# The last leftover sum of an attention and feed-forward kernel: its last step, its copy and its stores by halves of the columns

## The chip, the cores and the metric

The kernel runs on one core of a Trainium2 chip. The metric is the device time of one execution in microseconds (us); the text names the median of a few runs and, where the trace is read, the one execution that the profiler recorded. The engines are called as the profile calls them: PE (TensorE, the matrix products; PEld its weight loads), DVE (VectorE), ACT (ScalarE), POOL (GpSimd) and SP (SyncE). SP and ACT also issue transfers (DMAs), each on a hardware queue of its own: q1 is SP's, q10 is ACT's. The packets of both queues are carried by the core's 16 DMA engines. Below, an "engine" is a compute engine unless "DMA engine" is said.

## The reference

For each of 8 batches, attention over 32 memory slots makes a matrix x of 576 rows and 512 columns, and a two-layer feed-forward net follows on all 4608 rows:

```
x = attention(q, k, v, phi)          # 8 batches of 576 rows, 512 columns
h = x @ w_in                         # 2048 columns
g = 0.5 * h * (1 + erf(h / sqrt(2)))
out = g @ w_out                      # 4608 x 512, float32
```

## The kernel before

The second product, `g @ w_out`, sums over 2048 hidden columns in 16 steps f of 128 (`NF` = 16). Each step is three matmuls (`products`, L938), since g and w_out are each split in a high and a low part. The rows go in tiles of 128. From each half of a batch (288 rows), 256 rows go through `project_half`, and 32 rows are left over. The leftover rows of two batches, four blocks of 32, are gathered in the tile `tails` and make one tile of 128 rows: the leftover sum `tacc`, one bank of PSUM with 512 columns. It is made by `tail_split` (DVE splits `tails` in a high and a low part, four steps f at a time), `tail_project` (PE, 16 steps of three matmuls) and `tail_evict` (a copy of `tacc` from PSUM to the tile `to` in SBUF, and the stores of `to` to `out`). The last such sum, of batches 6 and 7 (b = B - 1 = 7), is the last work of the program: when its copy and its stores are done, the program ends.

In `out` the four blocks of 32 rows lie apart: block x starts at row (b - 1) * 576 + 288 x + 256, and a row is 2048 B. For b = 7 one 32-row store is issued for each block, in turn on ACT's and SP's queue (L1021). For b = 3 and b = 5 all four blocks go in one store (L1025), for b = 1 there are two stores of 64 rows (L1029). Another transfer that comes up below is the small load of `aT` (L473): it reads 64 rows as two blocks of columns, [2, 64, 128], from memory. The names `DMAHW0_49` and so on in the rows of the program's order are semaphores of transfers, `PE_49`, `DVE_49` and `Activation_49` those of the engines' work.

The order of the instructions on each engine is fixed by the program: a list written by hand, and then a plan.

Of the kernel before, what the change touches and what calls it, by code (L numbers as in the profile page):

```python
# [149 lines left out]
def slot_attention_gelu_ffn(  # L150
# [30 lines left out]
    nc = tc.nc  # L181
    P = 128
    B, G, _, S = phiT.shape
    M = 32
    D = P // 2
    NF, _, DM = w_in.shape
    DFF = NF * P
    HS = S // 2
# [41 lines left out]
    for x in PLACES.split():  # L230
        tag, size, n = x.replace("*", ":").split(":")
        sb.tile([P, int(size) // 4], F32, tag=tag, name=f"place_{tag}", bufs=int(n))

    def home(name):
        return {"tag": homes[name], "name": name, "bufs": 1}

    st = {"engine": None}

    def eng(usual):
        return {"d": nc.vector, "a": nc.scalar, "p": nc.gpsimd}[st["engine"] or usual]  # L240

    def copy(usual, dst, src):
        e = eng(usual)
        return e.copy(dst, src) if e is nc.scalar else e.tensor_copy(dst, src)  # L244
# [641 lines left out]
    def g_of(w, *k):  # L886

        dt, n = {"gf": (F32, 2), "gh": (F32R, 2), "gl": (F32R, 2)}[w]
        k = (w, *k)
        return tile_of(  # L890
            k, lambda: gs.tile([P, MAIN], dt, tag=w, name="_".join(map(str, k)), bufs=n)
        )
# [43 lines left out]
        nc.vector.tensor_copy(gh, x)  # L936
        nc.vector.tensor_tensor(gl, x, gh.bitcast(F32), op=ALU.subtract)

    def products(acc, f, gh, gl, first, last):
        for n, (x, w) in enumerate(((gh, wo_hi), (gh, wo_lo), (gl, wo_hi))):  # L940
            nc.tensor.matmul(  # L941
                acc, x, w[:, f, :], start=(first and n == 0), stop=(last and n == 2)
            )

    def project(b, f):
        _, _, first, last = steps[at_step[b, f]]
        if first:
            st["acc"] = [
                ps_acc.tile([P, DM], F32, tag=f"acc{j}", name=f"acc_{b}_{f}_{j}")
                for j in range(NT)  # L950
            ]
        acc = st["acc", b, f] = st["acc"]
        gh, gl = g_of("gh", b, f), g_of("gl", b, f)
        for j in range(NT):
            js = slice(j * P, (j + 1) * P)
            products(acc[j], f, gh[:, js], gl[:, js], first, last)

    def project_half(b, hf, i):
        if i == 0:
            st["acc", b, hf] = [  # L960
                ps_acc.tile([P, DM], F32, tag=f"acc{j}", name=f"acc_{b}_{hf}_{j}")
                for j in range(2)
            ]
        acc = st["acc", b, hf]
        gh, gl = g_of("gh", b, hf, i), g_of("gl", b, hf, i)
        for j in range(2):
            for x in range(2):
                js = slice((2 * x + j) * P, (2 * x + j + 1) * P)
                f = 2 * i + x
                products(acc[j], f, gh[:, js], gl[:, js], f == 0, f == NF - 1)  # L970
# [13 lines left out]
    def tail_project(b, k):  # L984
        if k == 0:
            st["tacc", b] = ps_acc.tile([P, DM], F32, tag="acc0", name=f"tacc_{b}")
        gh, gl = (g_of(w, "t", b, k) for w in ("gh", "gl"))
        for n in range(4):
            js = slice(n * P, n * P + P)
            f = 4 * k + n  # L990
            products(st["tacc", b], f, gh[:, js], gl[:, js], f == 0, f == NF - 1)

    def evict(b, j, f):

# [19 lines left out]

    def tail_evict(b):
        o = sb.tile([P, DM], F32, **home(f"to_{b}"))
        copy("a", o, st["tacc", b])
        if b == B - 1:
            for x in range(4):
                r = (b - 1) * S + x * HS + 2 * P  # L1020
                (nc.scalar, nc.sync)[x % 2].dma_start(out[r : r + M, :], o[M * x : M * x + M])  # L1021
            return
        if b > 1:
            rows = out[(b - 1) * S : (b + 1) * S].rearrange("(x s) n -> x s n", s=HS)
            nc.sync.dma_start(rows[:, 2 * P :], o)  # L1025
            return
        for x in range(2):
            r = (b - 1 + x) * S + MAIN
            nc.sync.dma_start(out[r : r + TL, :], o[TL * x : TL * x + TL])  # L1029
# [14 lines left out]
        "h": hidden, "gelu": gelu, "gh": gelu_hi, "gl": gelu_lo, "p": project, "o": evict, "os": store,  # L1044
        "P": project_half, "O": evict_half,
        "tg": tail_split, "tp": tail_project, "to": tail_evict,
    }
    st.update({("far", "pu", b, f): 1 for b in range(3, B) for f in (4, 12)})
# [27 lines left out]
    n = 2 * NF  # L1076
# [69 lines left out]
    for b, t in times.items():  # L1146
        x = 4 if b == 3 else b + 2
# [36 lines left out]
    first = {}  # L1184
# [46 lines left out]
    last = {}  # L1231
# [43 lines left out]
```

## Time and profile before

| | before |
|---|---|
| median of 3 runs | 699.79 us (699.37 to 701.95) |
| the profiled execution's own time | 700.24 us |
| its span, from the first instruction to the last | 698.5 us |
| PE busy | 684.2 us, 98% of the span |
| DVE, ACT, POOL busy | 54%, 43%, 6% |
| mean granted TensorE clock, share of full speed | 0.991 |
| bytes moved by DMA | 64.37 MB, mean 92 GB/s |

The profiled execution is 1.74 us longer than its span, and 0.45 us above the median. A change at the program's end moves the span's end by what it moves the last landing. Two measurements of this kernel can tell differences of about 0.5%, 3.5 us.

### The profile page before, as it was taken

To read this page: it belongs to the slowest core of one execution; us is meant where nothing else is said; L and a number is where in the kernel's file an instruction comes from. 1 tells how busy PE (TensorE), PEld (TensorE's weight loads), DVE (VectorE), ACT (ScalarE), POOL (GpSimd) and SP (SyncE) were. 2 spreads that over 40 slices of the span, in tenths; PEclk is the share of its full clock that TensorE was granted. 3 is DMA by queue.
4 is the path that set the end of the run, shared out by engine and by line. 5 is a ranking of instruction groups with operands and counts; after the bars stand their busy time and mean duration, and the time that the engine had idled before them with its cause. 6 is when DMAs were issued, how large, how long until landed. Compare 5 with 4: busy or idle time off the path is not lost.

```text
span 698.5 us, 12349 instructions
## 1 busy us (share of the span) xinstructions
PE 684.2 (98%) x4942; PEld 569.0 (81%) x4942; DVE 376.4 (54%) x695; ACT 301.3 (43%) x781; POOL 45.3 (6%) x38
## 2 busy tenths in 40 slices
PE   6799999999999999999999999999999999999997
PEld 5577887888768888888887888888878888888886
DVE  3999868854683555434844256334734246432222
ACT  5989658444652443615553234232531225332220
POOL 1333143300000000000000000000000000000000
PEclk9799999999999999999999999999999999999999
DMA  9973255322347260164501100030000200000001
GB/s 323 378 291 121 95 216 131 121 89 95 99 136 214 77 207 1 65 183 142 164 1 49 65 2 31 1 99 1 30 1 31 84 1 31 1 31 0 31 1 45
DMA packets 30717, 64.37 MB, mean 92 GB/s; under 512 B 3780, under 2 KB 8644, under 8 KB 30660
## 3 DMA queue, kind: packets, MB, share of 16 engines
q1 hardware_dynamic: 30564, 63.46, 27.3%
q8 instruction: 39, 0.64, 0.4%
q10 hardware_dynamic: 96, 0.13, 0.1%
q14 instruction: 18, 0.15, 0.1%
HBM read 54.13 MB, written 9.44 MB: 91 GB/s over the span
## 4 chain that ended last, share of the span: by engine, by line
PE 92%; DMA 4%; ACT 2%; SPq 1%; issue 0%; POOL 0%; ACTq 0%
PE acc L941 50%; PE h L901 28%; PE tacc L941 6%; PE pu L619 4%; DMA raw<-w_out 2%; DMA kv<-kv 1%; DMA raw<-w_in 1%; PE psc L619 1%; PE psc L536 1%; PE x L536 1%; ACT phi L432 0%; PE pt L457 0%; PE pk L536 0%; SPq L288 0%; ACT aT L244 0%
## 5 line engine op out<-in xcount | busy, mean ns | idle before, releaser
L901 PE MATMUL h<-p_hi,U 128*128 128x288 f32 x1024 | 202.1, 297 | 0.2 <-ACT tails L922 0.2
L941 PE MATMUL acc<-wo_hi,gh 128*128 128x512 f32 x512 | 201.0, 393 | 0.0
L941 PE MATMUL acc<-wo_lo,gh 128*128 128x512 f32 x512 | 199.6, 390 | 0.0
L941 PE MATMUL acc<-wo_hi,gl 128*128 128x512 f32 x512 | 199.5, 390 | 0.0
L913 ACT ACTIVATE gf<-h 128x256 f32<-128x256 f32 x192 | 74.0, 387 | 262.8 <-issue 182.2
L901 PEld LDWEIGHTS h<-p_hi,U 128*128 128x128 f32 x1024 | 163.3, 188 | 19.7 <-issue 7.3
L244 DVE CAST gh<-gf 128x512 fp32r<-128x512 f32 x106 | 45.0, 424 | 183.1 <-ACT gf L913 168.7
L941 PEld LDWEIGHTS acc<-wo_hi,gh 128*128 128x128 f32 x512 | 96.4, 188 | 23.9 <-issue 4.3
L941 PEld LDWEIGHTS acc<-wo_hi,gl 128*128 128x128 f32 x512 | 96.1, 188 | 20.9 <-DVE gl L928 0.5
L941 PEld LDWEIGHTS acc<-wo_lo,gh 128*128 128x128 f32 x512 | 96.1, 188 | 15.9
L901 PE MATMUL h<-p_lo,U 128*128 128x288 f32 x512 | 108.6, 294 | 0.0
L928 DVE TENSOR_TENSOR gl<-gf,gh 128x512 fp32r<-128x512 f32 x128 | 90.5, 708 | 24.1 <-ACT gh L244 14.8
L901 PEld LDWEIGHTS h<-p_lo,U 128*128 128x128 f32 x512 | 81.2, 188 | 0.2 <-DVE p_lo L739 0.2
L860 DVE TENSOR_TENSOR U<-pu,U 128x512 fp32r<-128x512 f32 (+2 forms) x50 | 40.8, 835 | 34.9 <-ACT U L244 34.7
L915 ACT ACTIVATE tails<-h 128x32 f32<-128x32 f32 x192 | 37.3, 194 | 0.0
L619 PE MATMUL pu<-w_in_sb,kT 64*32 64x512 f32 (+2 forms) x624 | 34.4, 528 | 1.0 <-ACT kT L244 0.6
L244 ACT CAST U<-pu 128x512 fp32r<-128x512 f32 (+2 forms) x43 | 28.9, 707 | 8.6 <-PE pu L619 7.4
L941 PE MATMUL tacc<-wo_hi,gh_t 128*128 128x512 f32 x64 | 25.3, 395 | 0.0
L941 PE MATMUL tacc<-wo_hi,gl_t 128*128 128x512 f32 x64 | 24.9, 390 | 0.0
L941 PE MATMUL tacc<-wo_lo,gh_t 128*128 128x512 f32 x64 | 24.9, 389 | 0.0
L342 POOL TENSOR_TENSOR y<-y,raw 128x512 int32<-128x512 int32 x14 | 18.8, 1346 | 58.4 <-DVE raw L318 25.3
L342 POOL TENSOR_TENSOR w_in_sb<-y,raw 128x512 int32<-128x512 int32 x14 | 20.4, 1465 | 29.3 <-DVE raw L318 8.0
(126 smaller groups left out, 571.5 us busy)
## 6 DMA issues: line engine op xcount, KB each, us to landing
kv<-kv SPq DMA_DIRECT2D x48, 256.0 KB, 5.7
out<-o SPq DMA_DIRECT2D x16, 512.0 KB, 4.4
raw<-w_out SPq DMA_DIRECT2D x14, 512.0 KB, 7.1
raw<-w_in SPq DMA_DIRECT2D x14, 512.0 KB, 9.7
q<-qT SPq DMA_DIRECT2D x9, 576.0 KB, 5.4
phi<-phiT SPq DMA_DIRECT2D x16, 288.0 KB, 3.5
aT<-phiN SPq DMA_DIRECT2D x6, 512.0 KB, 3.5
q<-qT SPq DMA_DIRECT2D x10, 288.0 KB, 8.6
```

The costliest lines, as they stand in the source:

```text
L244: return e.copy(dst, src) if e is nc.scalar else e.tensor_copy(dst, src)
L342: nc.gpsimd.tensor_tensor(w, y, low, op=ALU.add)
L536: nc.tensor.matmul(pk[32 * j : 32 * j + 32, : 2 * D], st["aT", b][:, c, g, 32 * j : 32 * j + 32], st["kv", b, g, c][:, :, j, :], start=(c ...
L619: nc.tensor.matmul(ps[g][M * j : M * j + M], st["kT", b][rows, t, M * j : M * j + M], moving[j][rows], start=True, stop=True,)
L860: nc.vector.tensor_sub(u[:, ..., 1, :], pu, u[:, ..., 0, :].bitcast(F32))
L901: i = nc.tensor.matmul(h[:, :HS], u[g][w], x[:, g, :], start=(n == 0), stop=(n == 3 * G - 1))
L913: nc.scalar.activation(gf[:, f % 2 * n : f % 2 * n + n], h[:, :n], AF.Gelu)
L915: nc.scalar.activation(t, h[:, n:HS], AF.Gelu)
L928: nc.vector.tensor_tensor(g_of("gl", *k), g_of("gf", *k), g_of("gh", *k).bitcast(F32), op=ALU.subtract)
L941: nc.tensor.matmul(acc, x, w[:, f, :], start=(first and n == 0), stop=(last and n == 2))
```

## The change

For b = 7 alone, three things are done by halves of the 512 columns (`COLS`). The last step f = 15 of the leftover sum is done as three matmuls on the left 256 columns and then three on the right. The copy is two copies, the left half by ACT and the right half by DVE. Behind each copy stand two stores, one on ACT's queue and one on SP's; a store covers 64 rows (two blocks of 32) and 256 columns. So four stores of 32 rows of 2048 B become four stores of 2 x 32 rows of 1024 B; the bytes are the same, 64 KB each.

```
-    def products(acc, f, gh, gl, first, last):
+    def products(acc, f, gh, gl, first, last, cs=slice(None)):
         for n, (x, w) in enumerate(((gh, wo_hi), (gh, wo_lo), (gl, wo_hi))):
             nc.tensor.matmul(
-                acc, x, w[:, f, :], start=(first and n == 0), stop=(last and n == 2)
+                acc, x, w[:, f, cs], start=(first and n == 0), stop=(last and n == 2)
             )
+
+    COLS = slice(0, DM // 2), slice(DM // 2, DM)
...
-            products(st["tacc", b], f, gh[:, js], gl[:, js], f == 0, f == NF - 1)
+            if b == B - 1 and f == NF - 1:
+                for cs in COLS:
+                    products(st["tacc", b][:, cs], f, gh[:, js], gl[:, js], False, cs is COLS[1], cs)
+            else:
+                products(st["tacc", b], f, gh[:, js], gl[:, js], f == 0, f == NF - 1)
...
     def tail_evict(b):
         o = sb.tile([P, DM], F32, **home(f"to_{b}"))
+        if b == B - 1:
+            for n, cs in enumerate(COLS):
+                copy("ad"[n], o[:, cs], st["tacc", b][:, cs])
+                for x in range(2):
+                    r = (b - 1 + x) * S
+                    rows = out[r : r + S].rearrange("(x s) n -> x s n", s=HS)
+                    (nc.scalar, nc.sync)[x].dma_start(
+                        rows[:, 2 * P :, cs], o[2 * M * x : 2 * M * x + 2 * M, cs]
+                    )
+            return
         copy("a", o, st["tacc", b])
-        if b == B - 1:
-            for x in range(4):
-                r = (b - 1) * S + x * HS + 2 * P
-                (nc.scalar, nc.sync)[x % 2].dma_start(out[r : r + M, :], o[M * x : M * x + M])
-            return
```

ACT's last rows of the program, as a difference (- before, + of the change; in brackets the semaphores that a row waits for; a DMA row shows the shape on the side of `out`):

```order
 L915 ACTIVATE tails<-h_1_15_6951 128x32
 L244 COPY o_1_6992<-acc_1_0_6752 128x512 [waits DMAHW4_49,PE_49]
-L244 COPY to_7057<-tacc_7000 128x512 [waits DMAHW5_49,PE_49]
-L1021 DMA out<-to_7057 32x512 [waits Activation_49]
-L1021 DMA out<-to_7057 32x512
-L1271 UNCONDITIONAL_BRANCH
+L244 COPY to_7060<-tacc_7000 128x256 [waits DMAHW5_49,PE_49]
+L1029 DMA out<-to_7060 2x32x256 [waits Activation_49]
+L1029 DMA out<-to_7060 2x32x256 [waits DVE_49]
+L1282 UNCONDITIONAL_BRANCH
```

ACT's copy covers half the columns, and its second store waits for DVE. The copy's wait on PE is for the last of the six matmuls: in the built program PE signals behind that one alone.

DVE's last rows of the changed program (before, its last row of work was the `gl_t_3` one):

```order
L936 CAST gh_t_2_7013<-tails 128x512 [waits PE_49]
L937 TENSOR_TENSOR gl_t_2_7014<-tails,gh_t_2_7013 128x512 [waits DVE_49,PE_49]
L936 CAST gh_t_3_7029<-tails 128x512 [waits PE_49,Activation_49]
L937 TENSOR_TENSOR gl_t_3_7030<-tails,gh_t_3_7029 128x512 [waits DVE_49,PE_49]
L244 COPY to_7060<-tacc_7000 128x256 [waits DMAHW5_49,Activation_49]
```

The new copy of the right half waits for ACT: for ACT's copy of the left half, which reads the same bank `tacc`.

SP's last stores of the changed program:

```order
L982 DMA out<-o_1_6439 128x2x512 [waits DVE_49,Activation_49]
L982 DMA out<-o_0_6725 128x2x512 [waits DMAHW5_49,DVE_49,Activation_49]
L982 DMA out<-o_1_6992 128x2x512 [waits DMAHW6_49,DVE_49,Activation_49]
L1029 DMA out<-to_7060 2x32x256 [waits DMAHW0_49,Activation_49]
L1029 DMA out<-to_7060 2x32x256 [waits DMAHW2_49,DVE_49]
```

Its two 32-row stores of before, `32x512`, are now two of shape `2x32x256`: the outermost count of the shape is 2 where it was 32.

## Rows read from the trace of the kernel before

**Rows 1.** The page's chain that ended last, by engine, share of the span

```profile
PE 92%; DMA 4%; ACT 2%; SPq 1%; issue 0%; POOL 0%; ACTq 0%
```

**Rows 2.** The chain in order of time, from 685 on: start us, us, what

```profile
684.86 9.53 PE tacc L941 x42
...
694.41 0.59 ACT to L244
```

**Rows 3.** Timeline of the end: start us, us, engine, line, operation

```profile
693.53 0.39 PE L941 MATMUL tacc<-wo_hi,gh_t 128*128 128x512 f32 x1
...
693.99 0.39 PE L941 MATMUL tacc<-wo_hi,gl_t 128*128 128x512 f32 x1
694.41 0.59 ACT L244 COPY to<-tacc 128x512 f32<-128x512 f32 x1 [11.65 <-PE tacc L941]
695.02 0.82 SPq L1021 DMA_DIRECT2D out<-to  x2
695.03 0.86 ACTq L1021 DMA_DIRECT2D out<-to  x2
```

**Rows 4.** Windows of the end; last three columns: PE clock, DMA share, GB/s

```profile
695.02:695.80 0.78, 0.00 (x0) 0.00 (x0) 0.00 (x0) 0.00 (x0) 0.00 (x0) 1.00 0.00 0
695.80:696.40 0.60, 0.00 (x0) 0.00 (x0) 0.00 (x0) 0.00 (x0) 0.00 (x0) 1.00 0.86 201
696.40:697.00 0.60, 0.00 (x0) 0.00 (x0) 0.00 (x0) 0.00 (x0) 0.00 (x0) 0.58 0.78 236
697.00:698.50 1.50, 0.00 (x0) 0.00 (x0) 0.00 (x0) 0.00 (x0) 0.00 (x0) 0.50 0.00 0
```

**Rows 5.** Timeline, PE at 668: matmuls of 288 columns, four merged

```profile
668.25 0.69 PE L901 MATMUL h<-p_hi,U 128*128 128x288 f32 x4
```

**Rows 6.** Groups by shape: copies of 256 columns from PSUM; busy us, mean ns

```profile
L244 ACT COPY sc<-psc_h 128x256 f32<-128x256 f32 x1 | 0.4, 372 | 0.8 <-PE psc_h L619 0.8
L244 DVE COPY sc<-psc_h 128x256 f32<-128x256 f32 x1 | 0.4, 425 | 0.2 <-PE psc_h L619 0.2
```

**Rows 7.** DMA view, 694.9 to 698.5: the packets of the last four stores

```profile
DMA packets 192, 0.26 MB, mean 73 GB/s; under 512 B 64, under 2 KB 64, under 8 KB 192
```

**Rows 8.** DMA view, 684 to 687: one store of 128 rows of `o`

```profile
DMA packets 272, 0.52 MB, mean 175 GB/s; under 512 B 16, under 2 KB 16, under 8 KB 272
...
out<-o SPq DMA_DIRECT2D x1, 512.0 KB
```

**Rows 9.** DMA view, 542 to 553: the store of `to` for b = 5, and three loads

```profile
DMA packets 565, 1.46 MB, mean 133 GB/s; under 512 B 52, under 2 KB 52, under 8 KB 564
...
q<-qT SPq DMA_DIRECT2D x1, 576.0 KB
q<-qT SPq DMA_DIRECT2D x2, 288.0 KB, 8.6
out<-to SPq DMA_DIRECT2D x1, 256.0 KB
```

**Rows 10.** SP's timeline: the small load of `aT` for b = 3

```profile
160.00 0.58 SPq L473 DMA_DIRECT2D aT<-phiN  x1
```

**Rows 11.** Windows in which few DMA engines are busy; last two columns: DMA share, GB/s

```profile
164.40:164.70 0.30, 0.30 (x3) 0.26 (x2) 0.00 (x0) 0.30 (x1) 0.00 (x0) 1.00 0.14 43
164.80:165.20 0.40, 0.40 (x3) 0.33 (x2) 0.00 (x0) 0.40 (x3) 0.00 (x0) 1.00 0.07 22
549.50:549.80 0.30, 0.30 (x3) 0.24 (x2) 0.11 (x1) 0.00 (x0) 0.00 (x0) 1.00 0.25 101
```

**Rows 12.** Durations of two issues: ns min/median/max, first and last start us

```profile
L1025 SPq DMA_DIRECT2D out<-to x2: 611/628/646, 380.7 to 542.7; - x2
L473 SPq DMA_DIRECT2D aT<-phiN x6: 557/574/662, 117.5 to 327.2; - x6
```

**Rows 13.** Windows behind an L1025 issue at 380.74; last two columns: DMA share, GB/s

```profile
380.74:382.00 1.26, 1.26 (x10) 1.18 (x9) 0.15 (x1) 1.14 (x4) 0.00 (x0) 1.00 0.00 0
382.00:382.50 0.50, 0.50 (x4) 0.42 (x3) 0.50 (x2) 0.50 (x3) 0.00 (x0) 1.00 0.39 45
```

## The prediction

> **What bounds the kernel now.** First the chain that ended last, by engine: PE is 92% of it [rows 1], so over the program only PE's work sets the time. The change is not there but at the very end, so next I read the chain in order of time: PE's leftover sum up to 694.39, one copy on ACT, and then nothing but transfers [rows 2]. The timeline shows that end piece by piece: the last matmul starts at 693.99 and takes 0.39, the copy of 512 columns starts at 694.41 and takes 0.59, and SP and ACT issue two stores each from 695.02 on, 0.82 and 0.86 us for the two [rows 3]. The windows show what the stores do: nothing moves until about 695.80, then 256 KB move in two stretches at 201 and 236 GB/s until 697.00, and in the last 1.50 us nothing moves (the writes' confirmation, SP's waits, the program's end) [rows 4]. No other work hides any of these 4.1 us: 0.6 copy, 0.8 until data flows, 1.2 data, 1.5 end. All else of the program keeps its place; so I cost the change in this stretch, against the profiled execution's span of 698.5 (its own time, 700.24, is 0.45 above the median of 699.79), and add the difference to the median.
>
> **The matmuls.** Three of 512 columns become six of 256, each with its weight load. The nearest row is the 288-column matmul: four in 0.69 us with a last one of about 0.29, so one starts every 0.13 us, with a load before each [rows 5]. 512 columns start every 0.23 (693.53 and 693.99 are two apart [rows 3]). On the line between the two, 256 columns start every 0.118 and end 0.28 after their start. The sixth ends at 693.53 + 5 x 0.118 + 0.28 = 694.40, against 693.99 + 0.39 = 694.38: +0.02.
>
> **The copies.** The left copy waits for all six matmuls and the right copy waits for the left one, so no copy overlaps PE, and the two run one after the other. ACT's copy of 256 columns out of PSUM took 0.37, DVE's 0.43 [rows 6]. Left: 694.43 to 694.80. First stores issued at 694.82, 0.20 earlier than now. Right: 694.82 to 695.25. The issue of a store with few row blocks took 0.57 to 0.63 [rows 12], longer than the 0.41 to 0.43 now, so each queue is free for its second store at 695.4 to 695.5: no earlier than now (695.43), and DVE's copy, ready at 695.25, is hidden behind the first issue.
>
> **The stores: on how many DMA engines?** This decides. A DMA leaves one small closing packet on each DMA engine that it used. The store of 128 rows has 256 pieces of 2 KB and 16 packets under 512 B: 16 DMA engines [rows 8]. The last four stores have 128 pieces, 64 other packets under 2 KB and the same 64 under 512 B: 16 each [rows 7]. The store for b = 5, whose shape on the side of `out` begins with 4 blocks (4x32x512), moves among three loads of 128 rows, and the stretch has 52 small packets: 3 x 16 + 4 [rows 9]. It ran on 4 DMA engines, although it has as many rows as the one on 16. The small load of `aT`, whose memory side begins with 2 blocks, is the last transfer issued before the windows at 164.4 and 164.8 [rows 10]: there the DMA share is 0.14, two sixteenths, at 43 GB/s, and then 0.07, one sixteenth, at 22 GB/s [rows 11]. It ran on 2. So the outermost count of the shape sets the number, and the new stores begin with 2 (2x32x256): I take 2 DMA engines for each.
>
> Their rate. One DMA engine moved 22 GB/s in pieces of 512 B, which is 23.5 ns for each; at a share of 0.25, four of them moved 101 GB/s, mostly in pieces of 2 KB [rows 11]: 25 each, 81 ns for 2048 B. No row has one moving 1 KB pieces to memory; bounds are half of 81 (40 ns) and twice 23.5 (47 ns); the line between the two sizes gives 42.7, which I take.
>
> Which two: no row names a DMA engine. All four stores have the same shape, and a split that follows from the shape alone puts them on the same pair; I take that. Then each of the two carries 128 pieces of 1 KB: 128 x 42.7 ns = 5.46 us (5.1 to 6.0), where the data takes 1.2 us now.
>
> The Trainium skill bears on this in "DMA: Bandwidth & Descriptors". Under "Why a DMA increments its semaphore by 16 and not by 1" it says that the count is the largest up to 16 that divides the outermost dimension (of size over 1) on both sides, and that a hardware queue takes the lowest-numbered ones; by that both queues' stores share one pair, and no run here shows which. Under "Specifications" it gives about 27 GiB/s for one DMA engine; by that the 128 KB of each would take 4.5 us and the sum below would be 703.3. The rows' 22 to 25 GB/s is lower, and the measurement decides.
>
> **The sum.** First stores issued 694.82. First data: behind the 4-block store nothing moved for 1.26 us [rows 13], behind today's 0.8 [rows 4]; the new form is nearer to the first, so 694.82 + 1.22 = 696.04 (bounds 695.6 and 696.1). The second stores are issued by 695.5, so their pieces are ready by 696.7, while the first two stores keep the pair busy until 698.77: no gap. Last data: 696.04 + 5.46 = 701.50, against 697.00. The end behind it keeps its 1.50: span 703.0, +4.5 us. From the median: 699.79 + 4.5 = **704.3 us** (the profiled execution alike would be 704.7). With the low bounds together: 695.6 + 5.1 = 700.7, +3.7, 703.5. With the high ones: 696.1 + 6.0 = 702.1, +5.1, 704.9. Spread of the runs adds about 0.4 on either side.
>
> **The rivals.** *A slow start of such stores.* In the first half microsecond of data of the 4-block store only 45 GB/s moved [rows 13] where its four could carry 101. If the new stores lose as much for their first 2 us or so, that is 2 x (1 - 45/101) = 1.1 us more, 705.4; if the whole transfer went at 45/101, 5.46 would be 12.3 and the time 711. For it: that store began so. Against: loads of 576 KB were issued right behind it, and nothing is issued behind ours; and today's last stores reach 201 GB/s at once [rows 4].
>
> *The stores fall on different pairs*, and the time is not slower by anything that can be told. If each queue has its own pair, each pair moves 64 pieces of 1 KB per DMA engine, 2.73 us from 696.04: last data 698.77, +1.8, 701.6. If each store has its own, the second ones move from 696.7 in 1.37 us: 698.05, +1.05, 700.8. It decides if the pair is given out by turns or by queue. Nothing in the rows speaks for it; that the count follows from the shape alone speaks against.
>
> *The stores still use 16 DMA engines*, because 64 rows on the tile's side count and not the 2. Then issues take 0.4 as now, the second stores are issued at 695.27, 0.16 earlier, and for each DMA engine 16 pieces at 42.7 ns stand in place of 8 at 81, 0.04 more: 699.7. Against it: the 4-block store has 128 rows on the tile's side and still used 4 [rows 9].
>
> **Chances.** The forecast (one pair, full rate) 0.68; one pair with a slow start 0.14; different pairs 0.10; 16 DMA engines 0.08. The likeliest gives 704.3, with a range of its own of 703.1 to 705.3 (its bounds and the runs' spread). The range to hold 8 in 10 takes the first case and all but the worst of the second, 703.0 to 706.3, and leaves out the last two cases, which hold 0.18. What a measurement can tell from no change is 3.5 us, so slower begins at 703.3: the first case is over it in nine of ten (0.61), the second always (0.14), so slower 0.75; the rest is the same but for a chance of 0.01 that something I don't see makes it faster.
>
> **What would show it.** In the profile after: the left copy at 694.4 with 0.37 and DVE's copy directly behind it with 0.43; first issues at 694.8, each near 0.6; in the DMA view of the last stretch 256 pieces of 1 KB and 8 packets under 512 B (64 if all 16 are used); in the windows a DMA share of 0.12 to 0.13 and about 48 GB/s for 5 us or more. A share of 0.25 means two pairs, one near 1 means 16. The forecast fails if the share is over 0.2, if the rate per DMA engine leaves 21 to 26 GB/s, or if the end behind the last data is not 1.5 us.

## The result and the profile after

The changed kernel took 707.36 us (median of 6 runs, 705.84 to 708.03) where the kernel before took 701.07 (median of 6, 699.37 to 703.43): a ratio of 1.0083 (of the means; the medians give 1.0090), 95% interval 1.0058 to 1.0109, so 4 to 8 us slower. The profiled execution took 705.84 with a span of 704.0, against 700.24 and 698.5.

The timeline of the changed kernel's end (the last matmul, the two copies, the issues; start us, us, engine):

```profile
693.96 0.28 PE L941 MATMUL tacc<-wo_hi,gl_t 128*128 128x256 f32 x1
694.28 0.37 ACT L244 COPY to<-tacc 128x256 f32<-128x256 f32 x1 [11.68 <-PE tacc L941]
694.68 1.16 SPq L1029 DMA_DIRECT2D out<-to  x2
694.68 1.94 ACTq L1029 DMA_DIRECT2D out<-to  x2
694.68 0.42 DVE L244 COPY to<-tacc 128x256 f32<-128x256 f32 x1 [4.81 <-ACT to L244]
```

It answers to [rows 3]. The copies stand as expected: ACT's left half takes 0.37 in place of 0.59, DVE's right half begins when it is done, not when PE is done ("<-ACT to"), and the first stores are issued at once behind the left copy. Then the windows, with the DMA share and GB/s in the last columns:

```profile
694.68:695.80 1.12, 0.00 (x0) 0.00 (x0) 0.42 (x1) 0.00 (x0) 0.00 (x0) 1.00 0.00 0
695.80:696.50 0.70, 0.00 (x0) 0.00 (x0) 0.00 (x0) 0.00 (x0) 0.00 (x0) 1.00 0.10 12
696.50:697.10 0.60, 0.00 (x0) 0.00 (x0) 0.00 (x0) 0.00 (x0) 0.00 (x0) 1.00 0.13 44
697.10:698.30 1.20, 0.00 (x0) 0.00 (x0) 0.00 (x0) 0.00 (x0) 0.00 (x0) 1.00 0.13 26
698.30:699.50 1.20, 0.00 (x0) 0.00 (x0) 0.00 (x0) 0.00 (x0) 0.00 (x0) 0.58 0.13 39
699.50:702.30 2.80, 0.00 (x0) 0.00 (x0) 0.00 (x0) 0.00 (x0) 0.00 (x0) 0.50 0.14 48
702.30:702.80 0.50, 0.00 (x0) 0.00 (x0) 0.00 (x0) 0.00 (x0) 0.00 (x0) 0.50 0.08 27
702.80:704.00 1.20, 0.00 (x0) 0.00 (x0) 0.00 (x0) 0.00 (x0) 0.00 (x0) 0.50 0.00 0
```

They answer to [rows 4]. The share never leaves 0.08 to 0.14 of 16, which is one to two DMA engines, while both queues are at work; the rate is 12 GB/s in the first 0.7 us, 26 to 44 up to 699.5, and 48 from there. The data takes 7.0 us (695.8 to 702.8) where it took 1.2. And the DMA view of 694 to 704, which answers to [rows 7]:

```profile
DMA packets 264, 0.26 MB, mean 26 GB/s; under 512 B 8, under 2 KB 264, under 8 KB 264
```

256 pieces of 1 KB and 8 closing packets, two for each of the four stores, where there were 64. Asked for shorter stretches, the same view tells whose pieces moved (q1 is SP's queue, q10 ACT's; packets, MB, share): first from 695.80 to 698.29, then from 698.36 to 699.68.

```profile
q1 hardware_dynamic: 64, 0.07, 12.0%
```

```profile
q10 hardware_dynamic: 53, 0.05, 13.3%
```

No packet of the other queue moved in either stretch. SP's first store moved its 64 pieces alone, and ACT's first store, whose issue took 1.37 us and was over at 696.05, moved nothing until SP's was through, as it would with one pair of DMA engines for both.

The work ahead of the end differs from execution to execution by some microseconds (ACT's last copy starts between 693.5 and 697.9 in the profiles of this study). So I compare the tail, from the start of ACT's last copy to the span's end: 4.1 us before (694.41 to 698.5), 9.7 after (694.28 to 704.0), +5.6. That agrees with the ratio (0.0083 x 701.07 = 5.8).

### The profile page after: what moved, and what is told of

It is laid out like the page before. It is cut to its first block, busy times and chain, and to the rows that moved or that the text cites. A ratio compares the mean times of both kernels' runs of the same rounds, so it can differ in the third digit from the quotient of the medians.

```text
span 704.0 us, 12358 instructions
## 1 busy us (share of the span) xinstructions
PE 683.3 (97%) x4945; PEld 568.3 (81%) x4945; DVE 376.6 (53%) x696; ACT 301.2 (43%) x781; POOL 45.3 (6%) x38
## 4 chain that ended last, share of the span: by engine, by line
PE 91%; DMA 4%; ACT 2%; SPq 1%; issue 0%; POOL 0%; DVE 0%; ACTq 0%
PE acc L941 49%; PE h L901 28%; PE tacc L941 6%; PE pu L619 4%; DMA raw<-w_out 2%; DMA kv<-kv 1%; DMA raw<-w_in 1%; PE psc L619 1%; PE psc L536 1%; PE x L536 1%; ACT phi L432 0%; PE pk L536 0%; SPq L288 0%; ACT aT L244 0%; PE pt L457 0%
## 5 line engine op out<-in xcount | busy, mean ns | idle before, releaser
L941 PE MATMUL tacc<-wo_hi,gh_t 128*128 128x512 f32 (+1 forms) x65 | 25.5, 392 | 0.0
L941 PE MATMUL tacc<-wo_hi,gl_t 128*128 128x512 f32 (+1 forms) x65 | 25.1, 386 | 0.0
L941 PE MATMUL tacc<-wo_lo,gh_t 128*128 128x512 f32 (+1 forms) x65 | 25.1, 386 | 0.0
L309 ACT ACTIVATE y<-raw 128x512 f32<-128x512 f32 x28 | 19.0, 679 | 8.8 <-DMA raw<-w_out 3.2
```

The costliest lines, as they stand in the source:

```text
L309: nc.scalar.activation(y, high.bitcast(F32), AF.Abs, scale=2.0**16)
L941: nc.tensor.matmul(acc, x, w[:, f, cs], start=(first and n == 0), stop=(last and n == 2))
```

## The experiments

**The shape of the stores, without the halves.** Only the stores of the kernel before are edited:

```
-            for x in range(4):
-                r = (b - 1) * S + x * HS + 2 * P
-                (nc.scalar, nc.sync)[x % 2].dma_start(out[r : r + M, :], o[M * x : M * x + M])
+            for x in range(2):
+                r = (b - 1 + x) * S
+                rows = out[r : r + S].rearrange("(x s) n -> x s n", s=HS)
+                (nc.scalar, nc.sync)[x].dma_start(rows[:, 2 * P :], o[2 * M * x : 2 * M * x + 2 * M])
```

> The kernel before, with one edit: the last copy of 512 columns is followed by two stores of two 32-row blocks each (2x32x512, pieces of 2 KB), one on each queue, in place of four stores of one block. No halves anywhere. Theory (the outermost count 2 puts each store on two DMA engines, the same two for both): 4 closing packets, DMA share 0.12 to 0.13, about 50 GB/s; each of the two carries 64 pieces of 2 KB at 80 ns, 5.1 us, and with the losses that the changed kernel shows at the start some 6 to 6.5 us of data; span 5 to 6 us above before, as the changed kernel. Rival (the pieces of 1 KB, the two copies in a row or the six matmuls cost the time): span within 0.5 us of before.

Measured: 707.01 us against 700.76 of the kernel before (27 runs on that chip), ratio 1.009 (1.0068 to 1.0111); tail 10.35 us, 6.2 over before. The DMA view and five windows, at the start, late in the data and behind it:

```profile
DMA packets 132, 0.26 MB, mean 24 GB/s; under 512 B 4, under 2 KB 4, under 8 KB 132
```

```profile
699.20:700.20 1.00, 0.00 (x0) 0.00 (x0) 0.00 (x0) 0.00 (x0) 0.00 (x0) 1.00 0.12 16
700.20:700.70 0.50, 0.00 (x0) 0.00 (x0) 0.00 (x0) 0.00 (x0) 0.00 (x0) 1.00 0.11 12
700.70:701.50 0.80, 0.00 (x0) 0.00 (x0) 0.00 (x0) 0.00 (x0) 0.00 (x0) 0.70 0.13 49
705.00:705.80 0.80, 0.00 (x0) 0.00 (x0) 0.00 (x0) 0.00 (x0) 0.00 (x0) 0.50 0.13 51
706.60:707.80 1.20, 0.00 (x0) 0.00 (x0) 0.00 (x0) 0.00 (x0) 0.00 (x0) 0.50 0.00 0
```

The whole loss is there with no halves, with pieces of 2 KB and one copy. The rival falls. The data took 7.4 us (699.2 to 706.6), more than the 6 to 6.5 expected.

**The halves, with stores of one block.** The changed kernel, with this in its place:

```
-                    rows = out[r : r + S].rearrange("(x s) n -> x s n", s=HS)
-                    (nc.scalar, nc.sync)[x].dma_start(
-                        rows[:, 2 * P :, cs], o[2 * M * x : 2 * M * x + 2 * M, cs]
-                    )
+                    for y in range(2):
+                        r = (b - 1 + x) * S + y * HS + 2 * P
+                        m = (2 * x + y) * M
+                        (nc.scalar, nc.sync)[x].dma_start(out[r : r + M, cs], o[m : m + M, cs])
```

> The changed kernel with its matmuls and copies by halves, but each half is stored by four stores of one 32-row block (32x256, pieces of 1 KB), two on each queue: eight stores in all. Theory (the outermost count): 16 DMA engines each, 128 closing packets, DMA share near 0.8, data over within 2 us of the first; four issues of about 0.4 us in a row on each queue, so the last is issued at about 1.2 us behind the first; span within 0.6 us of before (698 to 699.5). Rival (pieces of 1 KB or the halves cost it): span about 5 us above before.

Measured: 701.30 us, ratio 1.0011 (0.9997 to 1.0025); tail 4.41 us, 0.3 over before. 128 closing packets, and the data over in 1.9 us:

```profile
694.39:695.20 0.81, 0.00 (x0) 0.00 (x0) 0.42 (x1) 0.00 (x0) 0.00 (x0) 1.00 0.00 0
695.20:697.10 1.90, 0.00 (x0) 0.00 (x0) 0.00 (x0) 0.00 (x0) 0.00 (x0) 1.00 0.48 138
697.10:698.40 1.30, 0.00 (x0) 0.00 (x0) 0.00 (x0) 0.00 (x0) 0.00 (x0) 1.00 0.00 0
```

The share is 0.48, not the 0.8 that I expected. The DMA view of 694 to 698.4, in slices of 0.11 us (a digit is the share in tenths), shows four bursts, and each queue issues four stores in a row:

```profile
DMA  0000000000039613682167405840000000000000
```

That the 0.3 us come from these issues fits, but no run shows it by itself.

**The same four stores in one block.** The changed kernel, with only the rows of `out` changed:

```
-                    rows = out[r : r + S].rearrange("(x s) n -> x s n", s=HS)
                     (nc.scalar, nc.sync)[x].dma_start(
-                        rows[:, 2 * P :, cs], o[2 * M * x : 2 * M * x + 2 * M, cs]
+                        out[r + 2 * P : r + 2 * P + 2 * M, cs],
+                        o[2 * M * x : 2 * M * x + 2 * M, cs],
                     )
```

> The changed kernel; only the rows of out that a store writes differ: 64 rows in one block (64x256) in place of 2 blocks of 32, so half of the leftover rows land in other rows of out. Number of stores, bytes, pieces of 1 KB, copies, waits and issues are those of the changed kernel. Theory (the outermost count of the shape): 64 closing packets, DMA share near 0.8, issues of about 0.4 to 0.5 us, span 0 to 0.3 us below before's. Rival (two stores per half over 64 rows, or pieces of 1 KB, are slow as such): span 4 us or more above before.

Measured: 701.00 us, ratio 1.0000 (0.9989 to 1.0011); tail 4.23 us, 0.1 over before.

```profile
DMA packets 320, 0.26 MB, mean 62 GB/s; under 512 B 64, under 2 KB 320, under 8 KB 320
```

```profile
695.37:696.50 1.13, 0.00 (x0) 0.00 (x0) 0.42 (x1) 0.00 (x0) 0.00 (x0) 1.00 0.00 0
696.50:698.00 1.50, 0.00 (x0) 0.00 (x0) 0.00 (x0) 0.00 (x0) 0.00 (x0) 0.94 0.67 175
```

This is the cleanest of all: same instructions, same bytes and pieces, and the time differs by what one number in the shape does. It also shows what the halves would give with 16 DMA engines: nothing. The first data comes 1.13 us behind the first issue in place of 0.8, which takes back what the earlier issue gained: the share is 0.67 and the tail 0.1 over, where I expected about 0.8 and 0 to 0.3 under. So this delay doesn't need two blocks. It doesn't need 64 rows either: two versions below, with 32 rows in two blocks, have 1.2 and 1.3 us.

**One store of four blocks, nothing behind it.** This asks why the data was slow at its start. In the kernel before:

```
-            for x in range(4):
-                r = (b - 1) * S + x * HS + 2 * P
-                (nc.scalar, nc.sync)[x % 2].dma_start(out[r : r + M, :], o[M * x : M * x + M])
+            rows = out[(b - 1) * S : (b + 1) * S].rearrange("(x s) n -> x s n", s=HS)
+            nc.sync.dma_start(rows[:, 2 * P :], o)
```

> The kernel before with the last four stores made one, on SP, over four blocks (4x32x512, pieces of 2 KB), the shape that the store for b = 5 has, but with no load issued behind it. Theory (outermost count): 4 closing packets, 4 DMA engines with 32 pieces of 2 KB each at 80 ns, 2.6 us. On the slow start: if the loads behind the store for b = 5 made it slow, data flows at about 100 GB/s from its first half microsecond and the span is 1.8 us above before; if such a store starts slowly by itself, the first half microsecond shows about 45 GB/s again, the data takes 3 to 4 us and the span is 2.3 to 3.5 us above before.

Measured: 703.91 us, ratio 1.0042 (1.0029 to 1.0055); tail 7.2 us, 3.1 over before; 4 closing packets.

```profile
698.40:698.90 0.50, 0.00 (x0) 0.00 (x0) 0.00 (x0) 0.00 (x0) 0.00 (x0) 1.00 0.37 45
698.90:699.90 1.00, 0.00 (x0) 0.00 (x0) 0.00 (x0) 0.00 (x0) 0.00 (x0) 0.82 0.19 10
700.50:702.20 1.70, 0.00 (x0) 0.00 (x0) 0.00 (x0) 0.00 (x0) 0.00 (x0) 0.50 0.26 101
```

45 GB/s in the first half microsecond, as behind the store for b = 5 [rows 13], then 10, and only then the 101 of four DMA engines. So no load behind it is needed: such a store starts slowly by itself. The data took 4.2 us (698.4 to 702.6), a little over the 3 to 4 expected for that case.

**What makes the start slow.** Four edits of `blocks_full_width`, one run each: the two DMA engines of a store read partitions 16 apart, its two blocks lie 33 rows apart in `out`, both stores are on SP's queue, and a store reads every second partition.

```
+                s = 2 * P + x % 2 * 16                                    # blocks_16_rows_apart
+                (nc.scalar, nc.sync)[x % 2].dma_start(rows[:, s : s + 16], o[M * x : M * x + M])
...
+                rows = out[r : r + 66].rearrange("(y s) n -> y s n", s=33) # blocks_33_rows_apart_in_out
...
+                nc.sync.dma_start(rows[:, 2 * P :], o[2 * M * x : 2 * M * x + 2 * M])  # blocks_one_queue
...
+                m = x // 2 * 2 * M + x % 2                                # blocks_16_every_second_partition
+                (nc.scalar, nc.sync)[x % 2].dma_start(rows[:, s : s + 16], o[m : m + 2 * M - 1 : 2])
```

> As blocks_full_width (pieces of 2 KB, 64 for each of two DMA engines), but in four stores, two on each queue, each of two blocks of 16 rows (2x16x512): the two DMA engines of a store read partitions 16 apart in the tile, where they read partitions 32 apart before; the leftover rows land in another order in out. Closing packets: 8, DMA share 0.12 to 0.13 in all cases. Theory A for the slow start (two DMA engines that read partitions 32 apart in step get in each other's way on the tile's side): no slow start, 50 GB/s from the first half microsecond, data over in 5.2 to 5.5 us. Rival B (a store on few DMA engines starts slowly whatever it reads): under 25 GB/s in the first microsecond, data takes 6.5 to 7.5 us as in blocks_full_width.

> As blocks_full_width, but the two blocks of a store land 33 rows apart in out, not 288, so that half of the leftover rows go to other rows. Theory C for the slow start (the two streams of writes, 576 KiB apart in memory, get in each other's way there): no slow start, data over in 5.2 to 5.5 us. Theories A and B (it is on the tile's side, or of any such store): under 25 GB/s in the first microsecond and 6.5 to 7.5 us of data, as in blocks_full_width.

> As blocks_full_width, but both stores are issued on SP's queue, one behind the other. If the stalls come from the two queues (ACT's issue took 1.37 us beside SP's 0.54): no stalls, data over in 5.2 to 5.5 us. If they come from the store itself (theories A, B, C): data takes 6.3 to 7.5 us as in blocks_full_width.

> As blocks_16_rows_apart (four stores of 2x16x512, 16 pieces of 2 KB for each of two DMA engines in a store), but a store reads every second partition of 64, so that its two DMA engines read 32 partitions apart again; the leftover rows land in another order in out. Theory A (reading 32 apart in step is what is slow): the slow start lasts about 1.5 us as in blocks_full_width. Theory D (the slow start goes with what one store gives a DMA engine, 32 pieces there and 16 here): about 0.8 us as in blocks_16_rows_apart.

For each, the first 0.8 us of data and the 0.7 behind it; for `blocks_16_rows_apart` also the time from the first issue to the data, and the rest of the data. First `blocks_16_rows_apart`:

```profile
695.58:696.89 1.31, 0.00 (x0) 0.00 (x0) 0.00 (x0) 0.00 (x0) 0.00 (x0) 1.00 0.00 0
696.90:697.70 0.80, 0.00 (x0) 0.00 (x0) 0.00 (x0) 0.00 (x0) 0.00 (x0) 0.58 0.13 23
697.70:698.40 0.70, 0.00 (x0) 0.00 (x0) 0.00 (x0) 0.00 (x0) 0.00 (x0) 0.50 0.12 44
698.40:700.85 2.45, 0.00 (x0) 0.00 (x0) 0.00 (x0) 0.00 (x0) 0.00 (x0) 0.50 0.13 33
700.85:703.43 2.58, 0.00 (x0) 0.00 (x0) 0.00 (x0) 0.00 (x0) 0.00 (x0) 0.50 0.13 51
```

`blocks_33_rows_apart_in_out`:

```profile
696.42:697.22 0.80, 0.00 (x0) 0.00 (x0) 0.00 (x0) 0.00 (x0) 0.00 (x0) 1.00 0.14 18
697.22:697.92 0.70, 0.00 (x0) 0.00 (x0) 0.00 (x0) 0.00 (x0) 0.00 (x0) 1.00 0.10 12
```

`blocks_one_queue`:

```profile
699.65:700.45 0.80, 0.00 (x0) 0.00 (x0) 0.00 (x0) 0.00 (x0) 0.00 (x0) 1.00 0.14 18
700.45:701.15 0.70, 0.00 (x0) 0.00 (x0) 0.00 (x0) 0.00 (x0) 0.00 (x0) 1.00 0.08 9
```

`blocks_16_every_second_partition`:

```profile
695.28:696.08 0.80, 0.00 (x0) 0.00 (x0) 0.00 (x0) 0.00 (x0) 0.00 (x0) 1.00 0.12 23
696.08:696.78 0.70, 0.00 (x0) 0.00 (x0) 0.00 (x0) 0.00 (x0) 0.00 (x0) 1.00 0.14 50
```

Tails: 9.8, 10.3, 10.35 and 9.8 us; times of the one run each 706.56, 706.73, 709.99 and 705.04, against 701.42 (the last 701.27). The data took 6.5, 7.4, 7.3 and 6.7 us. 33 rows between the blocks in `out` in place of 288 change nothing (C falls), and one queue in place of two changes nothing. Both versions whose stores give a DMA engine 16 pieces are slow for 0.8 us, and those with 32 pieces for 1.5, whether the two DMA engines read 16 or 32 partitions apart: A falls, and D stands, for pieces of 2 KB. In the changed kernel, with 32 pieces of 1 KB, it is 0.7 us, so what counts may be the bytes that a store gives a DMA engine (32 KB twice, 64 KB) and not the number of pieces.

But D is about the start alone, and the start is not all that is lost. 64 pieces of 2 KB on each of the pair need 5.1 us at 80 ns, and with 16 pieces for each store the data still took 6.5. Of these 1.4 us some 0.4 went in the first 0.8 us, and most of the rest between 698.40 and 700.85, at 33 GB/s, while the first stores of the two queues were still on their way; from 700.85 on, the second stores moved at 51.

**One DMA engine.** The kernel before, with 31 rows a store:

```
-                (nc.scalar, nc.sync)[x % 2].dma_start(out[r : r + M, :], o[M * x : M * x + M])
+                (nc.scalar, nc.sync)[x % 2].dma_start(out[r : r + M - 1, :], o[M * x : M * x + M - 1])
```

> The kernel before with four stores of 31 rows in place of 32 (31x512; the last leftover row of each block isn't stored). 31 has no divisor up to 16 but 1: theory (the largest number up to 16 that divides the outermost count): 4 closing packets, one DMA engine for each store, and if all four fall on the same one, as the pair did, a DMA share of 0.06, 25 GB/s, and 124 pieces at 80 ns, 9.9 us of data; span 9 us or more above before. If the stores are spread, share 0.12 to 0.25 and 2.5 to 5 us. Rival (an odd count is cut as 32 is): as before. Slow start: theory A (two DMA engines hinder each other) says none with a single one: pieces of 80 ns from the first, 25 GB/s in the first microsecond; theory B or D (of the store itself): less than 15 GB/s in the first microsecond.

Measured: 709.68 us in its one run, against 701.27; tail 14.2 us, 10.1 over before.

```profile
DMA packets 128, 0.25 MB, mean 18 GB/s; under 512 B 4, under 2 KB 4, under 8 KB 128
```

```profile
695.10:696.10 1.00, 0.00 (x0) 0.00 (x0) 0.00 (x0) 0.00 (x0) 0.00 (x0) 1.00 0.07 14
696.10:697.70 1.60, 0.00 (x0) 0.00 (x0) 0.00 (x0) 0.00 (x0) 0.00 (x0) 0.81 0.06 9
697.70:706.50 8.80, 0.00 (x0) 0.00 (x0) 0.00 (x0) 0.00 (x0) 0.00 (x0) 0.50 0.07 26
```

One row less in each store costs 10 us. Four closing packets and a share of 0.06 to 0.07 from first to last: all four stores, of both queues, went through the same single DMA engine. It is slow for 2.6 us, with no second one to hinder it, and then at 26 GB/s. So a slow start doesn't take a pair. 2.6 us is more than the 1.5 us of the stores with 64 KB for a DMA engine, though here a store has 62 KB; the bytes of one store alone don't set the length.

No version tried is faster than the kernel before: the best of those with the halves had a tail 0.1 us longer, which can't be told from it.

## Why the prediction failed

The mechanism was the right one, and the forecast of slower held. Point by point:

- *Matmuls.* The six start 0.118 apart (693.37 to 693.96) and the last takes 0.28, as worked out.
- *Copies.* 0.37 and 0.42, one behind the other, stores issued 0.40 behind the start of the left copy (0.39 expected).
- *Issues.* SP's took 0.54 and 0.52, ACT's 1.37 and 0.53, where I had 0.57 to 0.63. It cost nothing: the pair had other pieces until the second stores came.
- *Two DMA engines for each store.* Right: 8 closing packets, share 0.13. *The same pair for all.* Right: the share never rises while both queues have stores open, ACT's first store moved nothing until SP's was through, and one DMA engine took all four in `one_dma_engine`. The Trainium skill's "DMA: Bandwidth & Descriptors" ("Why a DMA increments its semaphore by 16 and not by 1") says both, the count by the outermost dimension and the lowest-numbered ones; 2, 4 and 31 blocks or rows agree with the count (8, 4 and 4 closing packets for 4, 1 and 4 stores), and a common engine for both queues agrees with the second; which number it has, no run shows.
- *Rate.* 48 GB/s for the pair between 699.5 and 702.3, 42.7 ns for a piece of 1 KB on each: 1024 B x 2 / 48 GB/s, as taken from the line.
- *First data.* 1.12 to 1.2 us behind the first issue (1.22 expected).
- **"128 x 42.7 ns = 5.46 us" is the step that failed.** It takes the full rate from the first piece, and the data took 7.0 us. At 48 GB/s the 262 KB need 5.46. By the windows 1.3 of the 1.5 us more were lost up to 699.5, where 12 to 44 GB/s moved (0.5 in the first 0.7 us, 0.8 between 697.1 and 699.5), and 0.2 at the very end, at 27. So it is more than a slow start: the full rate failed over the first stores of both queues. I had part of this as the rival "a slow start", priced at 1.1 us, and gave it 0.14, because I took the slow half microsecond of [rows 13] to come from the loads behind that store. `one_store_of_4_blocks` shows it without any.
- *The end behind the last data* took 1.2, not 1.5: 0.3 back. The two together, 1.5 - 0.3 = 1.2 us, are nearly the 1.1 between the tail's +5.6 and the sum's +4.5. Two signs that the forecast named for its own failing came: this end, and a rate under 21 GB/s for a DMA engine (6 to 22 up to 699.5).
- **The time that it was added to** failed as well. 699.79 was the median of three runs, and six have 701.07, 27 others 700.76; I gave the runs 0.4 on either side. In parts of the whole, 704.3 / 699.79 = 1.0064 lies inside the measured interval (1.0058 to 1.0109); 699.79 + 5.6 = 705.4 would have been the rival's time, and 701.07 + 5.6 = 706.7 is within the runs of the changed kernel (705.84 to 708.03).

What stays open is why such stores move slowly at first. Shown: not by loads behind it, not by the distance of the blocks in memory (288 or 33 rows), not by the second queue, not by two DMA engines reading in step. With 32 KB for a DMA engine in each store the start was slow for 0.7 to 0.8 us, with 64 for 1.5. Against a rule made of the bytes alone stand `one_dma_engine` (62 KB, 2.6 us) and the store of `o` [rows 8]: it too gives each of its 16 DMA engines 32 KB, and it moves at 372 GB/s, 23 for each, from its first data:

```profile
685.10:686.50 1.40, 1.40 (x7) 1.14 (x7) 0.61 (x2) 0.00 (x0) 0.00 (x0) 1.00 0.95 372
```

That the pieces are taken as fast as they are made ready, and at the full rate only once they stand in line, would fit the second stores, which moved at the full rate; it wasn't tried. They can't be made ready at one rate for all stores, though: `o` moved its 256 pieces in 1.4 us, and the changed kernel 8 in its first 0.7. And the share in that slow stretch is 0.10, so the DMA engines are recorded as busy for most of it: each piece took longer.

## What to carry to other kernels

Before two stores are made one by a pattern with an outer loop of few blocks, look at the outermost count of the shape on the memory's side: 2, 4 or a prime such as 31 put the whole transfer on 2, 4 or one DMA engine here, and stores of both queues on the same ones. The closing packets in the DMA view (those under 512 B, divided by the transfers, where the pieces are larger) and the DMA share times 16 show it in any trace, also for transfers that are hidden today. At a program's end nothing hides it: there four stores with an outermost count of 32 beat two with a count of 2 by 6.2 us of tail and one with a count of 4 by 3.1, even at 0.4 us for each issue.

## What the runs showed that I had not expected

- Stores of 31 rows in place of 32 made the program's tail 10.1 us longer, through a single DMA engine at 26 GB/s. (The run's own expectation had 9 or more; I had not known it before this study.)
- Stores on few DMA engines start slowly: 12 GB/s on two in the changed kernel's first 0.7 us, 16 and 12 for 1.5 us with 2 KB pieces, 14 and 9 on one for 2.6 us. Later pieces of a queue's first store can be slow again (26 and 39 GB/s in the changed kernel).
- When SP and ACT issue such stores at the same moment, ACT's first issue takes longer: 1.37 us against SP's 0.54, in the changed kernel and in `blocks_full_width` alike. In `one_block_of_64`, with 64 rows in one block, ACT's first issue took 0.55. The lines are those of `blocks_full_width`:

```profile
698.06 0.54 SPq L1022 DMA_DIRECT2D out<-to  x1
698.06 1.37 ACTq L1022 DMA_DIRECT2D out<-to  x1
```
